# A fused retention and SiLU kernel: an early weight slice, and a two-deep pipeline for the first eight visits

## The chip, the cores and the metric

The kernel runs on one core of a Trainium2 chip. The metric is the device time of one execution in microseconds, the median of several runs. A profile of one execution gives the start and length of every instruction on the engines: TensorE (PE, with its weight loads as PEld), VectorE (DVE), ScalarE (ACT), GpSimd (POOL) and SyncE (SP), which here issues nearly all DMAs.

## The reference

Two stages follow each other. The first is a recurrent retention over 4 batches, 8 heads, 768 positions and a head dimension of 64. The second is a feed-forward layer over the resulting 3072 tokens.

```python
for t in range(S):
    state = gamma * state + k[:, :, t] (outer) v[:, :, t]
    y[:, :, t] = scale * q[:, :, t] @ state          # gamma depends on the head
x = y.transpose(0, 2, 1, 3).reshape(B * S, H * D)    # 3072 x 512
h = x @ w_in                                         # 512 x 2048
g = h * (1.0 / (1.0 + np.exp(-h)))
out = g @ w_out                                      # 2048 x 512
```

The weights arrive as 64-bit floating-point numbers, and the kernel converts them itself.

## The kernel before, in words

The recurrence is worked in chunks of 128 positions. A unit n is one chunk of one batch, in the order of chunks and within a chunk of batches, so there are 24 units, and units 0 to 3 make up chunk 0. Each unit passes through steps, and a "visit" m (the function `halves`) puts steps of several units together:

- `stage_t` (L403, L405): eight TensorE transposes of k and q, and two ScalarE copies (kt, qt) out of PSUM.
- `scale_k`: k is multiplied by its decay table gk. For units up to 5 this is one VectorE operation (L365). For units 6 to 13 it is eight ScalarE activations, one for each head (L354), since `2 * B - 3 < n < 3 * B + 2` with B = 4.
- `stage_s` (L419) and `stage_a` (L429): the state sums from scaled k and v, and the scores from kt and qt, both into the PSUM tile sc.
- `finish_a` and `scale_q`: VectorE masks the scores with the decay table (am, L437), forms mid and state (L446 or ScalarE's L444, and L450) and scales q (L370).
- `stage_y` (L462): y from the masked scores, then from the states in two halves. A small GpSimd memset stands as a fence between the halves.
- `finish_y`: ScalarE copies y out (L497) and forms the high part of x (L509). VectorE forms the two other parts (L512, L513).

In the program before, visit m holds `stage_t` and `scale_k` of unit m, the scores of unit m - 1 and y of unit m - 2: the pipeline is three deep. TensorE's order within a visit is transposes, the first part of y, sums, scores, the rest of y.

The feed-forward layer runs beside that. `product_in(c, f)` multiplies slice f of w_in (128 of its 2048 columns) with chunk c of x: twelve matmuls of 128x512 into two PSUM tiles ha and hb (L596). They use the three parts of the slice and the three parts of x, part after part. ScalarE copies ha out (L600), VectorE subtracts hb (L604), ScalarE applies Silu (L608), and g goes to DRAM.

A slice of w_in comes in three DMAs (`load_w`, L170 and L172) and is converted on its way. The 64-bit words go through ScalarE's L198 and VectorE's L200, L202, L205, L207, L209 and L215. After that come the three parts: ScalarE's L121, VectorE's L123, ScalarE's L125 and VectorE's L126. The staging tile has two buffers, so slice i + 2 can only be loaded once L209 of slice i has read its words. `take_w` converts a whole slice (slice 0 here). `begin_w` and `end_w` convert the later ones from visit 5 on, but not in visits 6 and 8. They are issued behind the newest mask:

```python
        if EARLY - 3 <= m < 3 * B + 2:
            with tc.issue_after(masked[0]):
                end_w()
                if m not in (EARLY - 2, EARLY):
                    begin_w()
```

The order of TensorE's instructions is that of the program. On the other engines a scheduler places the instructions, and each engine then works through its queue in that order. The first eight units (`EARLY = 2 * B`) are loaded at once, 24 DMAs of 256 KB each, with slices 0 and 1 between them. `make_identity`, `lag`, `decay`, `gk` and `gq` build tables on GpSimd and ScalarE at the start, some with many small memsets in `chunk_decays`.

After visit 10 has begun, the list `steps` sets the rest of the work: all further products of w_in with the remaining visits beside them, and then the products with w_out.

Of the kernel before, what the change touches and what calls it, by code (L numbers as in the profile page):

```python
# [18 lines left out]
ALU = mybir.AluOpType  # L19
# [14 lines left out]
def kernel(  # L34
# [28 lines left out]
    nc = tc.nc  # L63
    B, H, S, D = q.shape
# [65 lines left out]
    units = [(c, b) for c in range(NC) for b in range(B)]  # L130
    kqv = {"k": {}, "q": {}, "v": {}}
    EARLY = 2 * B

    FAR = 4 * B + 1
# [124 lines left out]
    for n in range(EARLY):  # L259
        for name in "kqv":  # L260
            load(name, n)
        if n in (1, 4):
            load_w(n // 4)


# [4 lines left out]
    for o in range(2):  # L270
        part = lag[ts(o, D), :D]
        nc.gpsimd.iota(part, pattern=[[1, D]], base=0, channel_multiplier=-1,
                       allow_small_or_imprecise_dtypes=True)
        nc.gpsimd.affine_select(out=part, in_=part, compare_op=ALU.is_ge, fill=1.0e6,
                                base=0, pattern=[[1, D]], channel_multiplier=-1)
    decay = const.tile([128, 2, HP, D], FP32, tag="decay", name="decay")
    for j in range(2):
        for a in range(HP):
# [24 lines left out]
    def first_chunk():  # L303
        nc.gpsimd.iota(lag, pattern=[[1, C]], base=1, channel_multiplier=0,
                       allow_small_or_imprecise_dtypes=True)
        for a in range(HP):
            nc.scalar.activation(out=gq[:, a, :], in_=lag, func=AF.Exp, scale=lgc[:, a : a + 1])

        nc.scalar.activation(out=token, in_=lgc[:1, :1], func=AF.Silu)
# [57 lines left out]
    def scale_q(n):  # L367
        c, b = units[n]
        t, g = (x if c > 0 else x[:, :, D:] for x in (qt[n], gq))
        nc.vector.tensor_tensor(out=t, in0=t, in1=g, op=ALU.mult)  # L370
# [25 lines left out]
    def stage_t(n):  # L396

        for name, to, bufs, src, tp in (
                ("kt", kt, 2, kqv["k"][n], turn(f"kp_{n}")),
                ("qt", qt, 3, kqv["q"].pop(n), banks("q", f"qp_{n}", 1)[:, 0])):  # L400
            tp = tp.rearrange("p (a t) -> p a t", a=HP)
            for a in range(HP):
                nc.tensor.transpose(tp[:, a, :], src[:, 2 * a : 2 * a + 2, :], ident)  # L403
            to[n] = one.tile([128, HP, C], FP32, tag=name, name=f"{name}_{n}", bufs=bufs)
            evac[:] = [nc.scalar.copy(out=to[n], in_=tp).ins]  # L405

    def score_tile(n):
        u = banks("s", f"sc_{n}")
        sc, sums = (u[:, :, ts(i, 4 * D)].rearrange("p o (a t) -> p o a t", a=HP)
                    for i in range(2))  # L410
        return sc, sums

    def stage_s(n, sums):

        kf, vs = kqv["k"].pop(n), kqv["v"][n]
        for a in range(HP):
            for o in range(2 if units[n][0] < NC - 1 else 1):
                for j in range(2):
                    nc.tensor.matmul(sums[ts(j, D), o, a, :], lhsT=kf[ts(o, D), 2 * a + j, :],  # L419
                                     rhs=vs[ts(o, D), 2 * a + j, :], start=True, stop=True,  # L420
                                     skip_group_check=True)

    def stage_a(n, sc):

        ktn = kt.pop(n)
        for a in range(HP):
            for o in range(2):
                for j in range(2):
                    nc.tensor.matmul(sc[ts(o, D), j, a, :], lhsT=ktn[ts(j, D), a, ts(o, D)],  # L429
                                     rhs=qt[n][ts(j, D), a, ts(o, D)], start=True, stop=True,  # L430
                                     skip_group_check=True)

    def finish_a(n, sc, sums):

        c, b = units[n]
        am[n] = one.tile([128, 2, HP, D], FP32, tag="am", name=f"am_{n}")
        mask = nc.vector.tensor_tensor(out=am[n], in0=sc, in1=decay, op=ALU.mult).ins  # L437
        masked[:] = [mask]
        mid = one.tile([128, HP, D], FP32, tag="mid", name=f"mid_{n}", bufs=2)
        steps_of[n] = state.get(b), mid  # L440

        with tc.issue_after(mask):
            if c == 0:
                nc.scalar.copy(out=mid, in_=sums[:, 0])  # L444
            else:
                nc.vector.tensor_tensor(out=mid, in0=state[b], in1=sums[:, 0], op=ALU.add)  # L446
            if c < NC - 1:
                state[b] = one.tile([128, HP, D], FP32, tag="state", name=f"state_{n}",
                                    bufs=B + 2)
                nc.vector.tensor_tensor(out=state[b], in0=mid, in1=sums[:, 1], op=ALU.add)  # L450

    def stage_y(n):

        vs, amn, qtn = kqv["v"].pop(n), am.pop(n), qt.pop(n)
        states = steps_of.pop(n)
        yp = banks("y", f"y_{n}")[:, :, : 4 * D].rearrange("p o (a t) -> p o a t", a=HP)

        started, done, new = set(), [], []

        def product(a, o, j, lhsT, rhs):  # L460
            e = j ^ (a % 2)
            i = nc.tensor.matmul(yp[ts(e, D), o, a, :], lhsT=lhsT, rhs=rhs,  # L462
                                 start=(e, o) not in started, stop=True,
                                 skip_group_check=True).ins
            started.add((e, o))
            if new:
                fence(done[-1], i)
                new.clear()
            done.append(i)

        def scores():
            for a in range(HP):
                for o in range(2):
# [12 lines left out]
        return scores, states_with, yp  # L486
# [53 lines left out]
    def visit(m):  # L540

        list(halves(m))

    def halves(m):

        first, mid, last = (0 <= m - i < len(units) for i in range(3))
        if first and m < FAR:
            stage_t(m)
        if last:
            scores, states_with, yp = stage_y(m - 2)  # L550
            scores()
            states_with(0)
        yield
        if mid:
            sc, sums = score_tile(m - 1)
            stage_s(m - 1, sums)
            stage_a(m - 1, sc)
            if 1 < m <= 3 * B + 1 and units[m - 1][1] == 0:
                next_chunk()

            with tc.issue_after(taken_out[0]) if m > 3 * B + 1 else ExitStack():
                finish_a(m - 1, sc, sums)
            scale_q(m - 1)
            if m > 3 * B + 1 and units[m - 1][1] == B - 1:

                behind_copy.append(next_chunk)
        if m == 0:
            chunk_decays()
            first_chunk()
        if first and m < FAR:  # L570
            scale_k(m)
        if last:
            states_with(1)
            finish_y(m - 2, yp)

        if FAR <= m < len(units):
            with tc.issue_after(fenced[0]):
                part_t(m)
        for name in "kqv":
            for n in (m + 1, m + 2):  # L580
                if n >= EARLY and n == (m + 1 if name == "v" or n > FAR else m + 2):
                    load(name, n)
# [28 lines left out]
    def put_g(keep):  # L611
        while len(pending) > keep:
            c, f, g = pending.pop(0)
            nc.sync.dma_start(out=g_dram[c, f], in_=g)
# [48 lines left out]
    ctx.enter_context(tc.manual_schedule(engines={mybir.EngineType.PE}))  # L663


    for m in range(EARLY + 1):
        visit(m)
        if m == 2:
            take_w()
        elif m == EARLY - 2:  # L670
            product_in(0, 0)
            load_w(3)
        elif m == EARLY:
            product_in(0, 1)
            put_g(1)
    half_visits = (x for m in range(EARLY + 1, 3 * B + 1) for x in chain(halves(m), (None,)))
    next(half_visits)
    product_in(0, 2)
    put_g(1)
    next(half_visits)  # L680
    next(half_visits)

    half = NF // 2
# [55 lines left out]
    for c in range(NC):  # L739
# [8 lines left out]
        for f in range(NF):  # L748
            n = c * NF + f
# [62 lines left out]
```

## Time and profile before

| | |
|---|---|
| time, median of 3 runs | 629.17 us (628.28 to 629.5) |
| span of the profiled execution | 625.6 us, 13502 instructions |
| ScalarE's first and VectorE's first operation with data | 2.09 us and 7.65 us |
| first product, (0,0), on TensorE | 36.24 to 39.27 us |
| second and third, (0,1) and (0,2) | 48.77 to 51.78 and 53.44 to 56.46 us |
| transposes of unit 10 | 57.71 us |

In the lines below a number of microseconds from the start of the span comes first, then the length, the engine, the line of the program, the operation and its tiles. In tables of stretches, each engine's busy time stands with its number of instructions. Where a line ends in brackets, these give how long the engine was idle before, and what it waited for last.

### The profile page before, as it was taken

To read this page: it belongs to the slowest core of one execution; us is meant where nothing else is said; L and a number is where in the kernel's file an instruction comes from. 1 tells how busy PE (TensorE), PEld (TensorE's weight loads), DVE (VectorE), ACT (ScalarE), POOL (GpSimd) and SP (SyncE) were. 2 spreads that over 40 slices of the span, in tenths; PEclk is the share of its full clock that TensorE was granted. 3 is DMA by queue.
4 is the path that set the end of the run, shared out by engine and by line. 5 is a ranking of instruction groups with operands and counts; after the bars stand their busy time and mean duration, and the time that the engine had idled before them with its cause. 6 is when DMAs were issued, how large, how long until landed. Compare 5 with 4: busy or idle time off the path is not lost.

```text
span 625.6 us, 13502 instructions
## 1 busy us (share of the span) xinstructions
PE 604.0 (97%) x5384; PEld 497.1 (79%) x5384; DVE 422.5 (68%) x729; ACT 319.5 (51%) x611; POOL 22.5 (4%) x79
## 2 busy tenths in 40 slices
PE   5888999999999999999999999999999999999997
PEld 3777787888888888888787888888788888888885
DVE  2898998698889877766698795644635453644631
ACT  6688896666665556765566871412221221313211
POOL 3000000000000211111000000000000000000000
PEclk9899999999999999999999999999999999999999
DMA  9998886446558899989566673432524432433201
GB/s 201 205 216 205 230 222 200 166 151 200 206 161 233 246 244 239 253 225 264 198 236 204 205 228 104 150 119 85 179 74 131 140 102 101 148 122 110 93 1 68
DMA packets 137999, 107.32 MB, mean 172 GB/s; under 512 B 94800, under 2 KB 103248, under 8 KB 137936
## 3 DMA queue, kind: packets, MB, share of 16 engines
q1 hardware_dynamic: 135056, 101.21, 57.4%
q10 hardware_dynamic: 2880, 5.24, 2.3%
q8 instruction: 42, 0.69, 0.5%
q14 instruction: 21, 0.17, 0.1%
HBM read 66.06 MB, written 36.70 MB: 164 GB/s over the span
## 4 chain that ended last, share of the span: by engine, by line
PE 84%; DVE 5%; SPq 5%; DMA 2%; ACT 2%; issue 1%; DVEq 0%; ACTq 0%; POOLq 0%
PE ha L596 25%; PE o L761 21%; PE oa L761 14%; PE hb L596 12%; PE ob L761 7%; SPq L150 4%; PE y L462 3%; PE sc L419 1%; PE sc L429 1%; DMA wf<-in_moe_w_out_dram 1%; DMA wf<-in_moe_w_in_dram 1%; DMA kqv<-in_k_dram 1%; DVE g L604 1%; DVE xt L512 1%; DVE cs L205 1%
## 5 line engine op out<-in xcount | busy, mean ns | idle before, releaser
L596 PE MATMUL ha<-xt,wi 128*128 128x512 f32 x768 | 193.1, 393 | 1.1 <-DVE g L604 1.0
L596 PEld LDWEIGHTS ha<-xt,wi 128*128 128x128 f32 x768 | 142.1, 188 | 32.7 <-DVE g L604 2.3
L761 PE MATMUL o<-wo,gs 128*128 128x512 f32 x576 | 146.3, 389 | 0.0
L761 PEld LDWEIGHTS o<-wo,gs 128*128 128x128 f32 x576 | 108.1, 188 | 22.4
L653 DVE TENSOR_TENSOR gs<-gr,gs 128x512 fp32r<-128x512 f32 x96 | 62.3, 686 | 85.8 <-ACT gs L651 85.8
L651 ACT ACTIVATE gs<-gr 128x512 fp32r<-128x512 f32 x96 | 53.5, 621 | 128.3 <-issue 123.6
L761 PE MATMUL oa<-wo,gs 128*128 128x512 f32 x384 | 118.4, 389 | 0.0
L596 PE MATMUL hb<-xt,wi 128*128 128x512 f32 x384 | 102.9, 390 | 0.4 <-ACT g L600 0.4
L604 DVE TENSOR_TENSOR g<-g,hb 128x512 f32<-128x512 f32 x96 | 65.7, 684 | 45.6 <-ACT g L600 29.5
L596 PEld LDWEIGHTS hb<-xt,wi 128*128 128x128 f32 x384 | 71.9, 188 | 16.0 <-ACT g L600 1.1
L761 PEld LDWEIGHTS oa<-wo,gs 128*128 128x128 f32 x384 | 72.0, 188 | 15.3 <-ACT o L769 0.3
L608 ACT ACTIVATE g<-g 128x512 f32<-128x512 f32 x96 | 60.6, 631 | 43.7 <-DVE g L604 43.3
L761 PE MATMUL ob<-wo,gs 128*128 128x512 f32 x192 | 75.3, 392 | 0.3 <-DVE o L770 0.3
L600 ACT ACTIVATE g<-ha 128x512 f32<-128x512 f32 x96 | 56.9, 592 | 29.7 <-PE ha L596 22.1
L654 DVE SCALAR_TENSOR_TENSOR gs<-gs 128x512 fp32r<-128x512 f32 x96 | 62.3, 684 | 0.1
L761 PEld LDWEIGHTS ob<-wo,gs 128*128 128x128 f32 x192 | 36.0, 188 | 9.4 <-DVE o L770 2.1
L198 ACT ACTIVATE ca<-wf 128x512 f32<-128x512 f32 x32 | 21.6, 674 | 10.4 <-DVE cs L205 5.6
L209 DVE SCALAR_TENSOR_TENSOR cp<-wf,cp 128x512 f32<-128x512 uint32 x32 | 22.8, 712 | 0.6
L769 ACT ACTIVATE o<-o 128x512 f32<-128x512 f32 x10 | 6.0, 600 | 33.4 <-PE o L761 33.0
L205 DVE SCALAR_TENSOR_TENSOR cs<-ca,cs 128x512 uint32<-128x512 uint32 x32 | 22.1, 691 | 0.8
L462 PE MATMUL y<-qt,mid 64*64 64x64 f32 x384 | 20.6, 222 | 0.0
L770 DVE TENSOR_TENSOR o<-o,o 128x512 f32<-128x512 f32 x10 | 6.8, 688 | 19.3 <-ACT o L769 19.3
(85 smaller groups left out, 568.5 us busy)
## 6 DMA issues: line engine op xcount, KB each, us to landing
gd<-g SPq DMA_DIRECT2D x96, 256.0 KB, 3.1
gr<-gd SPq DMA_DIRECT2D x96, 256.0 KB, 2.7
wf<-in_moe_w_out_dram SPq DMA_DIRECT2D x16, 512.0 KB, 4.6
out_dram<-o ACTq DMA_DIRECT2D x20, 256.0 KB, 2.1
wf<-in_moe_w_in_dram SPq DMA_DIRECT2D x16, 256.0 KB, 3.8
wf<-in_moe_w_in_dram SPq DMA_DIRECT2D x32, 128.0 KB, 3.9
kf<-in_k_dram SPq DMA_DIRECT2D x16, 256.0 KB, 5.1
qf<-in_q_dram SPq DMA_DIRECT2D x16, 256.0 KB, 3.7
```

What stands on the lines that cost most here:

```text
L150: nc.sync.dma_start(out=t, in_=src[b, :, ds(c * C, C)].rearrange("h t d -> t h d"))
L205: nc.vector.scalar_tensor_tensor(out=s, in0=a, scalar=3, in1=s, op0=ALU.logical_shift_left, op1=ALU.bitwise_or)
L209: nc.vector.scalar_tensor_tensor(out=p.bitcast(FP32), in0=lo, scalar=2.0 ** -52, in1=p.bitcast(FP32), op0=ALU.mult, op1=ALU.mult)
L462: i = nc.tensor.matmul(yp[ts(e, D), o, a, :], lhsT=lhsT, rhs=rhs, start=(e, o) not in started, stop=True, skip_group_check=True).ins
L596: nc.tensor.matmul(hb if i == 2 else ha, lhsT=w_sb[f][:, i, ts(kk, 128)], rhs=xt[c][:, i, kk, :], start=kk == 0 and i != 1, stop=kk == KIN ...
L600: copied[:] = [nc.scalar.activation(out=hs, in_=ha, func=AF.Copy, scale=ONE_E).ins]
L604: taken_out[:] = [nc.vector.tensor_tensor(out=hs, in0=hs, in1=hb, op=ALU.subtract).ins]
L608: nc.scalar.activation(out=hs, in_=hs, func=AF.Silu)
L651: nc.scalar.activation(out=t[:, 0, :], in_=g, func=AF.Copy, scale=HALF)
L653: nc.vector.tensor_tensor(out=t[:, 1, :], in0=g, in1=high, op=ALU.subtract)
L654: nc.vector.scalar_tensor_tensor(out=t[:, 2, :], in0=t[:, 1, :].bitcast(FP32), scalar=-1.0 / EPS, in1=high, op0=ALU.mult, op1=ALU.add)
L761: nc.tensor.matmul(o, lhsT=g, rhs=wo[f][:, i, :], start=first_ and i != 1, stop=last and i != 0)
```

## The change

The change reorders the start of the kernel, and the arithmetic stays as it is.

- Slice 0 of w_in is loaded behind unit 0 instead of behind unit 1, and its conversion (`take_w`) is issued after visit 0 instead of after visit 2.
- The decay tables' last input (`lagged`) is put ahead of the many memsets on GpSimd.
- For units 4 to 7 transposes and scores lie in one visit, and y comes in the visit after: two deep instead of three. A visit without a unit of its own (`at_once(None, 3, 2)`) makes the step from three to two. `soon` places `scale_k` directly behind the transposes in these visits. Visits 8 and 9 go back to three deep.
- The first products stand in visit 5 (behind the transposes, ahead of y), visit 8 (between its halves) and visit 9 (at its end). They were behind visit 6, behind visit 8 and between the halves of visit 9.

The purpose is to have x of chunk 0 ready, and the first product running, sooner. From the first half of visit 10 on, TensorE's order is the same in both programs.

```diff
-        if n in (1, 4):
+        if n in (0, 4):
             load_w(n // 4)
...
-        nc.gpsimd.affine_select(out=part, in_=part, compare_op=ALU.is_ge, fill=1.0e6,
-                                base=0, pattern=[[1, D]], channel_multiplier=-1)
+        lagged = nc.gpsimd.affine_select(out=part, in_=part, compare_op=ALU.is_ge, fill=1.0e6,
+                                         base=0, pattern=[[1, D]], channel_multiplier=-1).ins
...
+    def steps_at(m, ms=None, my=None, behind_t=None):
...
+        soon = mid and ms == m or m is None
         if first and m < FAR:
             stage_t(m)
+            if soon or m == 1:
+                scale_k(m)
+        if behind_t:
+            behind_t()
...
         if m == 0:
-            chunk_decays()
-            first_chunk()
-        if first and m < FAR:
+            with tc.issue_after(lagged):
+                chunk_decays()
+                first_chunk()
+        if first and m < FAR and not soon and m != 1:
             scale_k(m)
...
-    for m in range(EARLY + 1):
-        visit(m)
-        if m == 2:
-            take_w()
-        elif m == EARLY - 2:
-            product_in(0, 0)
-            load_w(3)
-        elif m == EARLY:
-            product_in(0, 1)
-            put_g(1)
-    half_visits = (x for m in range(EARLY + 1, 3 * B + 1) for x in chain(halves(m), (None,)))
-    next(half_visits)
+    at_once(0)
+    take_w()
+    at_once(1, 0)
+    at_once(2, 1, 0)
+    at_once(3, 2, 1)
+    at_once(None, 3, 2)
+    at_once(4, 4, 3)
+    at_once(5, 5, 4, lambda: product_in(0, 0))
+    at_once(6, 6, 5)
+    load_w(3)
+    at_once(7, 7, 6)
+    eighth = steps_at(8, None, 7)
+    next(eighth)
+    product_in(0, 1)
+    put_g(1)
+    list(eighth)
+    at_once(9, 8)
     product_in(0, 2)
     put_g(1)
-    next(half_visits)
+    half_visits = (x for m in range(EARLY + 2, 3 * B + 1) for x in chain(halves(m), (None,)))
     next(half_visits)
```

More of the change, by code (lines that the diff above doesn't have):

```diff
@@ L544, in halves @@
     def halves(m):
-        first, mid, last = (0 <= m - i < len(units) for i in range(3))
+        return steps_at(m, m - 1, m - 2)
+    def steps_at(m, ms=None, my=None, behind_t=None):
+        first, mid, last = (n is not None and 0 <= n < len(units) for n in (m, ms, my))
+        soon = mid and ms == m or m is None
         if first and m < FAR:
             stage_t(m)
+            if soon or m == 1:
+                scale_k(m)
+        if behind_t:
+            behind_t()
         if last:
-            scores, states_with, yp = stage_y(m - 2)
+            scores, states_with, yp = stage_y(my)
             scores()
@@ L554, in halves @@
         if mid:
[L555 to L558, printed above, removed]
+            sc, sums = score_tile(ms)
+            stage_s(ms, sums)
+            stage_a(ms, sc)
+            if 0 < ms <= 3 * B and units[ms][1] == 0:
                 next_chunk()
[L561 to L564, printed above, removed]
+            with tc.issue_after(taken_out[0]) if ms > 3 * B else ExitStack():
+                finish_a(ms, sc, sums)
+            scale_q(ms)
+            if ms > 3 * B and units[ms][1] == B - 1:
                 behind_copy.append(next_chunk)
         if m == 0:
-            chunk_decays()
-            first_chunk()
-        if first and m < FAR:
+            with tc.issue_after(lagged):
+                chunk_decays()
+                first_chunk()
+        if first and m < FAR and not soon and m != 1:
             scale_k(m)
@@ L573, in halves @@
             states_with(1)
-            finish_y(m - 2, yp)
+            finish_y(my, yp)
+        if m is None:
+            return
         if FAR <= m < len(units):
@@ L663, with at_once @@
     ctx.enter_context(tc.manual_schedule(engines={mybir.EngineType.PE}))
-    for m in range(EARLY + 1):
-        visit(m)
-        if m == 2:
-            take_w()
-        elif m == EARLY - 2:
-            product_in(0, 0)
-            load_w(3)
-        elif m == EARLY:
-            product_in(0, 1)
-            put_g(1)
-    half_visits = (x for m in range(EARLY + 1, 3 * B + 1) for x in chain(halves(m), (None,)))
-    next(half_visits)
+    def at_once(*of, **kw):
+        list(steps_at(*of, **kw))
+    at_once(0)
[15 more added lines that the diff above has]
+    at_once(9, 8)
     product_in(0, 2)
     put_g(1)
-    next(half_visits)
+    half_visits = (x for m in range(EARLY + 2, 3 * B + 1) for x in chain(halves(m), (None,)))
     next(half_visits)
```

## The prediction

> **What bounds the kernel now.** I read the page first, then the busy time by stretch, then the engines' timelines between 20 and 66 us. The page says what kind of kernel this is:
>
> ```profile
> PE 604.0 (97%) x5384; PEld 497.1 (79%) x5384; DVE 422.5 (68%) x729; ACT 319.5 (51%) x611; POOL 22.5 (4%) x79
> PE   5888999999999999999999999999999999999997
> DVE  2898998698889877766698795644635453644631
> ```
>
> TensorE is full from about 65 us to the end; no other engine is. So only the time at which TensorE reaches that full stretch can move the result, and whatever is won or lost before it is carried to the end. The stretches show where TensorE still has holes (columns: stretch, length, busy us and instructions of PE, weight loads, VectorE, ScalarE, GpSimd, then granted clock, DMA share, GB/s):
>
> ```profile
> 10.00:20.00 10.00, 7.71 (x193) 6.79 (x192) 5.88 (x12) 4.47 (x10) 0.09 (x1) 0.83 1.28 218
> 20.00:30.00 10.00, 7.46 (x263) 6.42 (x264) 9.48 (x19) 7.60 (x18) 0.18 (x2) 1.00 0.91 199
> 30.00:36.00 6.00, 5.00 (x227) 4.38 (x223) 5.04 (x11) 5.59 (x16) 0.35 (x2) 1.00 1.01 225
> 36.00:43.00 7.00, 7.00 (x174) 5.85 (x163) 6.93 (x14) 5.58 (x15) 0.09 (x1) 1.00 0.85 210
> 43.00:50.00 7.00, 4.06 (x136) 3.40 (x136) 6.13 (x13) 6.31 (x17) 0.09 (x1) 1.00 0.82 172
> 50.00:57.00 7.00, 7.00 (x116) 5.64 (x118) 4.79 (x10) 6.51 (x17) 0.09 (x1) 1.00 0.81 218
> 65.00:75.00 10.00, 10.00 (x185) 8.18 (x176) 9.45 (x18) 8.76 (x21) 0.09 (x1) 1.00 0.84 226
> ```
>
> The holes are before 65 us, and there VectorE (9.48 of 10, 6.93 of 7) and ScalarE (5.59 of 6, 6.31 of 7, 6.51 of 7) are nearly full. VectorE is empty mainly before 12 us. The timeline gives the marks against which I count: the scores of unit 6 masked on VectorE (mask 6 from here on) at 42.79 and those of unit 7 (mask 7) at 49.21, the third slice of w_in converted from 44.66 to 54.16, and the transposes of unit 10, the first work after which both programs issue the same instructions on TensorE, at 57.71:
>
> ```profile
> 33.85 2.03 ACT L354 ACTIVATE kqv<-kqv,gk 128x64 f32<-128x64 f32 x8
> 42.79 0.69 DVE L437 TENSOR_TENSOR am<-sc,decay 128x512 f32<-128x512 f32 x1
> 44.66 0.42 DVE L200 TENSOR_SCALAR cs<-wf 128x512 uint32<-128x512 uint32 x1
> 49.21 0.68 DVE L437 TENSOR_TENSOR am<-sc,decay 128x512 f32<-128x512 f32 x1
> 53.48 0.68 DVE L126 SCALAR_TENSOR_TENSOR wi<-wi,wil 128x512 fp32r<-128x512 f32 x1
> 56.97 0.69 DVE L604 TENSOR_TENSOR g<-g,hb 128x512 f32<-128x512 f32 x1 [2.21 <-ACT g L600]
> 57.71 0.66 PE L403 MATMUL kp<-ident,kf 128*128 128x128 f32 x4
> ```
>
> The first of these lines matters most below: the eight ScalarE scalings of k of unit 6 take 2.03 us, and today nobody waits for them, because the score product of unit 6 is a whole visit later.
>
> **What the Trainium skill says.** "Perfetto Trace Analysis", Per-engine timelines: VectorE, ScalarE and GpSimd are strict FIFO. The trace agrees: VectorE sits 2.21 us before 56.97 with other work queued behind. So an operation's place in its queue decides, and I use the instruction order of the changed program. "ScalarE: Activation LUTs", What ACT_TABLE_LOAD costs: an activation with one pointer operand costs about 280 ns + 0.833 ns an element, back-to-back ones overlapping by 93 ns; for 64 elements an estimate of 0.24 us, eight of them 1.9 us. The trace has 2.03 us, which I use. "DMA: Bandwidth & Descriptors", Why small descriptors are slow: 256-byte descriptors lose some 27%. The k, q, v rows are 256 bytes; the trace shows 199 to 225 GB/s here.
>
> **The change, part by part.** Durations are differences between consecutive starts: 0.60 us for a 128x512 VectorE operation, 0.33 for 128x256 and for the tensor-scalars; 0.47 to 0.60 for a ScalarE copy of 512; 0.95 for a unit's transposes, 0.75 and 0.38 for the two halves of y, 0.46 for the state sums, 0.42 for the scores, 2.72 for a product of 12 matmuls (2.72 us per product in the full stretch); 0.15 to 0.2 between engines.
>
> First slice and decay tables early. Removed: nothing; the bytes are the same. Slice 0 (0.5 MB, 2.3 us at 228 GB/s) passes unit 1, whose k then lands near 10.1 instead of 7.6 us. VectorE's first instruction becomes slice 0's L200, near 8.9 (today its first is unit 0's scaling at 7.65). Unit 0's scores end near 14.3 instead of 11.9 because the transposes of unit 1 stand ahead of them. Unit 2 lands at 13.2 and 14.5 as today. The tables move from 4.0 to about 2.2 on ScalarE, but the copies of unit 0 still wait for its q (6.38), so that is worth nothing. Queue order then gives mask 0 at 14.4, mask 1 at 20.4 (slice 0's L123 stands ahead of it), mask 2 at 24.4, mask 3 at 27.4, mask 4 at 31.1. Today: 12.6, 19.4, 23.6, 27.2, 31.65. So at mask 4 the change is 0.6 ahead, with unit 5 not yet transposed. The early slice pays almost nothing: VectorE idles until unit 0's scores anyway.
>
> First product at visit 5. Transposes of unit 5 at 31.0 (its q landed by 29). The product waits for x of unit 3: y3 ends 31.05, two ScalarE operations, then 33.0, VectorE's two parts ready at 33.7 and 34.9. It runs 33.0 to 35.95, against 36.24 to 39.27 today: 3.2 us earlier. But it stands ahead of y4 and of unit 5's scores, so VectorE waits for its end (34.8 to 36.1) and for the scores (36.7 to 37.95), 2.5 us that today it spends on slice 1. Mask 5 is at 37.95 (today 37.32).
>
> Visits two deep. A unit's scores now follow its transposes in the same visit, so the copy of k and q and the scaling of k lie on the path. For units up to 5 the scaling is one VectorE operation; for 6 and 7 it is ScalarE's eight. Visit 6: transposes 37.95 to 38.9; ScalarE copies until 40.3, scalings until 42.2; scores end 42.9 (visible 43.0); mask 6 stands behind slice 1's L215: 44.1 (today 42.79). Visit 7: transposes 43.2; ScalarE runs y5, a copy, x5, slice 1's L121, a copy, three scalings until 46.8, slice 1's L125 (waits for L123, 47.3) until 47.9, five scalings until 49.2; scores end 49.95; mask 7 at 50.05 (today 49.21), VectorE empty for 1.6 us before it. TensorE waits about 2.2 us for unit 6's scalings and 3.2 us for unit 7's, with no work beside them (today it loses about 2.5 us here to instruction stalls, in the trace put down to issue): y7, both products and two units' transposes are queued behind.
>
> Slice 2. Its conversion is held behind the newest mask; in visit 7 that was mask 6, now it is mask 7. L200 is at 51.95 instead of 44.66, L215 ends at 56.3. Behind it in ScalarE's queue its L121 also stands after the Silu and x7: 58.3 to 58.95, L125 to 60.5, L126 on VectorE to 60.95. Product (0,1) runs 51.85 to 54.6 (today 48.77 to 51.78); transposes and scores of unit 8 and 9 end at 56.85; product (0,2) then waits 2.1 us for slice 2 and runs 59.1 to 62.45. So unit 10's transposes come at 62.4 instead of 57.71: +4.7 us.
>
> The DMA order hides itself: slice 3 waits for slice 1's L209 (43.5 instead of 37.4), and k, q, v of units 8 to 10 queue behind it, landing by about 51 and 57.5, before their uses at 56 and 62.4. Behind unit 10 all is as before; TensorE is full, and only a few tenths of its later waits (0.3 to 0.4 at 300 to 342 us) can take any back. I take off 0.5 for these and for small errors on one side: +4.2 us, 633.4 us.
>
> **Rivals.** (a) VectorE alone decides. The work up to product (0,2)'s subtraction is the same 42.9 us of VectorE steps in both programs (three slices at 4.28, eight units at 3.06, two extra scalings 1.2, unit 8's 1.86, three subtractions 1.8, 0.7 of slice 3); today that is done at 61.4. Started at 8.9 and with only 6 us of holes it would be done at 57.8: 3.6 us faster, 625.6. For it: VectorE is the fullest engine from 20 to 45. Against: the holes I count above sum to 9 us or more. (b) ScalarE is nimbler than laid out and slice 2's wait vanishes: only visits 6 to 9 lag, +2.6 less 0.5, 631.3. For it: it is a sum of many small steps; against: the queue order is fixed. (c) The loads decide: they fill the DMA engines until 46 us in both programs (shares 0.82 to 1.28); then nothing changes, 629.2. Against: today's waits of TensorE for k and q are 4.1 us in all, most of them before 15 us.
>
> **How the numbers follow.** Main case 0.50 at 633.4; (b) 0.20 at 631.3; (c) 0.08 at 629.2; (a) 0.22 at 625.6, the other side. The main case runs to 636 if the instruction stalls of 0.5 to 1.5 us that TensorE shows today (idle put down to issue, 2.8 us on y) fall on the path too. Faster 0.22, same 0.08, slower 0.70. Range 626.0 to 636.0.
>
> **What would show it.** Right: ScalarE's scalings of units 6 and 7 end last before the state sums; mask 7 at or after 49 us, slice 2's L200 after 50 us, a TensorE wait for ScalarE's L121 before the third product, unit 10's transposes near 62 us. Wrong: mask 7 near 45 us, VectorE without holes between 30 and 50 us, unit 10's transposes before 57 us; then (a) holds.

## The result, and the profile after

| | before | after |
|---|---|---|
| time, median of 4 runs each, taken together | 628.72 us (627.94 to 629.5) | 635.07 us (634.05 to 636.01) |
| ratio after / before | | 1.011, 95% interval 1.0085 to 1.0134 |
| span of the profiled execution | 625.6 us | 634.2 us |
| first product on TensorE | 36.24 us | 34.66 us |
| mask 7 | 49.21 us | 51.84 us |
| slice 2, first VectorE step (L200) | 44.66 us | 53.71 us |
| third product on TensorE | 53.44 us | 61.60 us |
| transposes of unit 10 | 57.71 us | 65.03 us |

The change makes the kernel slower by 6.9 us by the ratio (1.1% of 628.72); the two medians lie 6.35 us apart. The purpose was met in the letter: the first product does start 1.6 us sooner. But the third starts 8.2 us later, and the end follows the third.

In the program after, the first product line of the code is L608 (L596 before), the copy and the subtraction of g are L612 and L616, and Silu is L620. The page has the same number of instructions on every engine as before:

```profile
PE 608.0 (96%) x5384; PEld 499.7 (79%) x5384; DVE 423.6 (67%) x729; ACT 319.1 (50%) x611; POOL 21.9 (3%) x79
PE   5688999999999999999999999999999999999997
DVE  2877899778979887777678797463645544554631
```

Nothing was added to any engine's work (VectorE is busy for 423.6 us against 422.5), and from the fifth slice of the span on TensorE is as full as before. So the loss lies at the start. But TensorE's busy time has grown, from 604.0 to 608.0 us: up to the transposes of unit 10 it is 47.05 of 65.03 us, against 43.33 of 57.71 us before. Of the 7.3 us between these two marks only about half is idle time. In the rest, the same instructions take longer, at a lower clock or where they follow another engine's work piece by piece (both below). The stretches say where (columns as before: stretch, length, then busy us and instructions of PE, weight loads, VectorE, ScalarE, GpSimd, then granted clock, DMA share, GB/s):

```profile
30.00:36.00 6.00, 4.13 (x110) 3.47 (x102) 5.12 (x11) 4.97 (x12) 0.09 (x1) 1.00 0.99 213
36.00:43.00 7.00, 5.73 (x190) 4.67 (x192) 4.58 (x10) 4.32 (x11) 0.09 (x1) 1.00 0.71 167
43.00:50.00 7.00, 5.02 (x162) 4.10 (x152) 6.90 (x13) 5.22 (x15) 0.18 (x2) 1.00 0.58 144
50.00:57.00 7.00, 6.99 (x133) 6.02 (x134) 5.24 (x12) 5.98 (x19) 0.09 (x1) 0.76 0.83 184
57.00:65.00 8.00, 7.00 (x106) 5.22 (x106) 5.98 (x10) 7.26 (x18) 0.00 (x0) 1.00 0.78 197
```

Between 36 and 43 us VectorE is busy for 4.58 us where it was busy for 6.93, and ScalarE for 4.32 instead of 5.58: TensorE, VectorE and ScalarE wait for each other in turn. One other thing stands in these lines: TensorE's clock is 0.76 in 50 to 57 us (it was 1.00). The timeline has the marks:

```profile
34.66 2.11 PE L608 MATMUL ha<-xt,wi 128*128 128x512 f32 x8 [0.77 <-ACT xt L509]
41.92 2.02 ACT L354 ACTIVATE kqv<-kqv,gk 128x64 f32<-128x64 f32 x8
45.91 0.68 DVE L437 TENSOR_TENSOR am<-sc,decay 128x512 f32<-128x512 f32 x1
49.63 1.29 ACT L354 ACTIVATE kqv<-kqv,gk 128x64 f32<-128x64 f32 x5
50.01 1.24 PE L419 MATMUL sc<-kqv 64*64 64x64 f32 x19 [1.15 <-ACT kqv L354]
51.84 0.69 DVE L437 TENSOR_TENSOR am<-sc,decay 128x512 f32<-128x512 f32 x1 [1.57 <-PE sc L429]
53.71 0.42 DVE L200 TENSOR_SCALAR cs<-wf 128x512 uint32<-128x512 uint32 x1
60.93 0.62 ACT L121 ACTIVATE wi<-cs 128x512 fp32r<-128x512 f32 x1
61.60 1.20 PE L608 MATMUL ha<-xt,wi 128*128 128x512 f32 x4 [0.71 <-ACT wi L121]
65.03 0.60 PE L403 MATMUL kp<-ident,kf 128*128 128x128 f32 x4
```

Read from the bottom: unit 10's transposes follow the third product, which waited for slice 2's L121 on ScalarE. That conversion began on VectorE at 53.71, behind mask 7 at 51.84. Mask 7 waited 1.57 us for the scores, these stand behind the state sums in TensorE's order, and the sums waited 1.15 us for ScalarE's scalings of k. The scalings of unit 6 take 2.02 us (2.03 before), but now the sums of the same visit need them.

A caution on single profiles, each of which is one execution. The profile after is of the slowest of its four (636.01 us). The times lie 1.8 us above the spans, so that before is of an execution of some 627.4 us, about 1 us below the median. Therefore the spans differ by 8.6 us where the medians differ by 6.35. The transposes of unit 10 also move by some 3 us with the clock that the execution was granted (experiment 1). So below the ratios decide how much, and the profiles show which wait.

The clock itself is a rival that no experiment holds fixed. The record has the mean granted clock of every execution, and one minus this clock, times the span, is an estimate of the most that half clock can have cost (where TensorE waits anyway, it costs nothing). Averaged over the executions of each program it comes to about 2 us before, 2.2 to 2.9 us in the experiments that are three deep throughout (1, 9 and 11), 5.2 us in the change, and 3.3 to 6.9 us in the others. So up to some 3 us of the loss may be the lower clock that comes after waits, and not the waits themselves.

### The profile page after: what moved, and what is told of

It is laid out like the page before. It is cut to its first block, busy times and chain, and to the rows that moved or that the text cites. A ratio compares the mean times of both kernels' runs of the same rounds, so it can differ in the third digit from the quotient of the medians.

```text
span 634.2 us, 13499 instructions
## 1 busy us (share of the span) xinstructions
PE 608.0 (96%) x5384; PEld 499.7 (79%) x5384; DVE 423.6 (67%) x729; ACT 319.1 (50%) x611; POOL 21.9 (3%) x79
## 4 chain that ended last, share of the span: by engine, by line
PE 80%; DVE 7%; DMA 5%; ACT 5%; issue 2%; SPq 0%; DVEq 0%; ACTq 0%; POOLq 0%
PE ha L608 22%; PE o L781 20%; PE oa L781 14%; PE hb L608 11%; PE ob L781 7%; PE y L462 3%; PE sc L429 1%; DMA qw<-qp 1%; PE sc L419 1%; DVE g L616 1%; DMA gd<-g 1%; DMA wf<-in_moe_w_out_dram 1%; PE qp L403 1%; DVE cp L209 1%; PE kp L403 1%
## 5 line engine op out<-in xcount | busy, mean ns | idle before, releaser
L608 PE MATMUL ha<-xt,wi 128*128 128x512 f32 x768 | 193.4, 394 | 3.2 <-DVE g L616 1.0
L608 PEld LDWEIGHTS ha<-xt,wi 128*128 128x128 f32 x768 | 142.1, 188 | 35.5 <-DVE g L616 2.4
L608 PE MATMUL hb<-xt,wi 128*128 128x512 f32 x384 | 103.3, 391 | 0.4 <-ACT g L612 0.2
L616 DVE TENSOR_TENSOR g<-g,hb 128x512 f32<-128x512 f32 x96 | 65.6, 684 | 48.7 <-ACT g L612 35.9
L608 PEld LDWEIGHTS hb<-xt,wi 128*128 128x128 f32 x384 | 71.7, 188 | 16.8 <-ACT g L612 1.8
L620 ACT ACTIVATE g<-g 128x512 f32<-128x512 f32 x96 | 60.5, 630 | 44.6 <-DVE g L616 44.4
L612 ACT ACTIVATE g<-ha 128x512 f32<-128x512 f32 x96 | 56.7, 590 | 33.5 <-PE ha L608 19.8
L437 DVE TENSOR_TENSOR am<-sc,decay 128x512 f32<-128x512 f32 x24 | 16.5, 686 | 9.6 <-PE sc L429 9.6
```

What stands on the lines that cost most here:

```text
L608: nc.tensor.matmul(hb if i == 2 else ha, lhsT=w_sb[f][:, i, ts(kk, 128)], rhs=xt[c][:, i, kk, :], start=kk == 0 and i != 1, stop=kk == KIN ...
L612: copied[:] = [nc.scalar.activation(out=hs, in_=ha, func=AF.Copy, scale=ONE_E).ins]
L616: taken_out[:] = [nc.vector.tensor_tensor(out=hs, in0=hs, in1=hb, op=ALU.subtract).ins]
L620: nc.scalar.activation(out=hs, in_=hs, func=AF.Silu)
```

## The experiments

Each ratio is to the program before on the same chip. The change itself stands at 1.0110 (1.0085 to 1.0134), that is +6.9 us. From these intervals, a difference between the change and an experiment is uncertain by nearly 2 us.

**1. The early slice alone.** The program before with slice 0 behind unit 0, its conversion after visit 0, and the tables ahead of the memsets. The pipeline is three deep everywhere.

```diff
-        if n in (1, 4):
+        if n in (0, 4):
...
-        if m == 2:
+        if m == 0:
             take_w()
```

> The visits, products and their order of the kernel before, three deep, with only the early slice 0 (load behind unit 0, conversion after visit 0) and the decay tables put ahead. Theory (the early slice pays almost nothing, since VectorE is empty until unit 0's scores anyway): within 1 us of the kernel before, 628 to 630 us, unit 10's transposes within 1 us of 57.7. Rival (VectorE's early start is worth what it frees later): 3 us faster, unit 10's transposes at 55 us or sooner.

Measured: 628.73 us against 628.32, ratio 1.0005 (0.9994 to 1.0016). The early slice and the early tables cost 1.0 us at most and bring 0.4 us at most. The mark was a miss: unit 10 is transposed at 61.07 us, 3.4 later than in the profile of the program before. The profiled execution took 630.03 us, 1.3 above the median of this run. TensorE's clock in it is 0.50 from 47 to 53 us, where the profile before has 1.00; with the edges it is 6.8 us at half, which is 3.4 us of work lost. In the waits of its TensorE from 20 to 66 us (engine, line, what it waited for: total us, times, longest) little but instruction stalls and the wait for ys is left, beside two waits of 0.3 and 0.2 us:

```profile
PE y L462 <- issue: 4.6, 4, 1.5
PE y L462 <- ACT ys L497: 2.3, 1, 2.3
PE qp L403 <- issue: 1.8, 1, 1.8
```

The 2.3 us for ys are at the place where slice 0's L121 and L125 now stand ahead in ScalarE's queue. The wait is real, and the ratio says that the end does not feel it here.

**2. The scalings of k of units 6 and 7 on VectorE.** One operation in place of eight activations.

```diff
-            if 2 * B - 3 < n < 3 * B + 2:
+            if 2 * B - 1 < n < 3 * B + 2:
```

> The changed kernel, with k of units 6 and 7 scaled by one VectorE operation each instead of eight ScalarE activations. Theory (the ScalarE scalings stand on the path of the two-deep visits): TensorE no longer waits for L354 before the state sums of unit 7, which end near 49 instead of 51.3 us; unit 10's transposes near 63 instead of 65.0; about 2 us faster than the changed kernel, near 633. Rival (the order of the loads or the place of the first product is the cause): no gain, and 1.2 us more of VectorE work to pay, 635 to 636.

Measured: 633.16 us against 628.32, ratio 1.0075 (1.0055 to 1.0094). The time is as expected, but the interval overlaps that of the change. TensorE still waits for the scalings, on the other engine:

```profile
PE sc L419 <- DVE kqv L365: 2.3, 2, 1.8
```

VectorE's queue was not empty in front of the scaling either, so the wait was moved, and only part of it removed.

**3. Slice 2 begun a visit sooner.** It is begun behind mask 6 again, and slice 3's load is issued ahead of it.

```diff
-                if m not in (EARLY - 2, EARLY):
+                if m not in (EARLY - 1, EARLY):
...
-    at_once(6, 6, 5)
     load_w(3)
+    at_once(6, 6, 5)
```

> The changed kernel, with the conversion of slice 2 begun in visit 6, behind mask 6, instead of in visit 7, behind mask 7. Theory (slice 2 comes late for the third product): L200 of slice 2 near 50 instead of 53.7 us, TensorE's waits for L121 and L125 before the third product (1.0 us together) gone, 1 to 1.5 us faster than the changed kernel, near 634. Rival: the time lies in the visits alone, no gain, 635.

Measured: 632.29 us against 628.32, ratio 1.0068 (1.0048 to 1.0088), whose upper end just meets the interval of the change. The gain is more than was expected. Slice 2's L200 is at 50.26 us, unit 10 at 63.83, and the third product no longer waits for the slice at all. The wait for slice 2 was part of the loss; experiment 6 shows it apart from the change.

**4. Both of these.** The edits of 2 and 3 together.

> Both edits together: k of units 6 and 7 scaled on VectorE and slice 2 begun in visit 6. Theory: the gains add, 3 to 4 us faster than the changed kernel, 631 to 632, unit 10's transposes near 61. Rival (VectorE is the bound once the waits are gone): no more than the better one of the two alone, 633.

Measured: 634.47 us against 628.32, ratio 1.0097 (1.0079 to 1.0114). This is a miss: it is no better than either edit alone. VectorE's timeline shows a cause (L123 and L126 belong to slice 1, L200 to slice 2, L365 is the scaling of unit 7):

```profile
49.54 0.68 DVE L123 SCALAR_TENSOR_TENSOR wil<-cs,wi 128x512 f32<-128x512 f32 x1
50.15 0.68 DVE L513 SCALAR_TENSOR_TENSOR xt<-xt 128x512 fp32r<-128x512 f32 x1
50.75 0.68 DVE L126 SCALAR_TENSOR_TENSOR wi<-wi,wil 128x512 fp32r<-128x512 f32 x1
51.35 0.42 DVE L200 TENSOR_SCALAR cs<-wf 128x512 uint32<-128x512 uint32 x1
51.69 0.68 DVE L365 TENSOR_TENSOR kqv<-kqv,gk 128x512 f32<-128x512 f32 x1
...
54.80 0.68 DVE L437 TENSOR_TENSOR am<-sc,decay 128x512 f32<-128x512 f32 x1
```

With slice 2 begun a visit sooner, VectorE's queue holds conversion steps of both slices ahead of unit 7's scaling. The scaling waits behind work for products of the next visits, and TensorE behind the scaling: in the waits of this run it is 4.1 us for L365, where experiment 2 had 2.3. Mask 7 comes at 54.80 us, later than in the change itself. A second cause is not excluded: in this profile TensorE is at half clock for some 10 us between 43 and 58 us, while in experiment 2's the clock stays at 1.00 from 30 to 65 us. Over all executions the estimate from the mean clock is 6.9 us here, against 4.6 and 4.8 us in experiments 2 and 3.

**5. The scalings on GpSimd.** The rival was that VectorE's queue, with slice 2 behind mask 7, is the only cause, and that the scalings don't matter. If they do, and it is queues that hold them up, an engine with an empty queue must do better.

```diff
-            if 2 * B - 3 < n < 3 * B + 2:
+            if 2 * B - 1 < n < 3 * B + 2:
...
-            nc.vector.tensor_tensor(out=t, in0=t, in1=g, op=ALU.mult)
+            on = nc.gpsimd if 2 * B - 3 < n < 2 * B else nc.vector
+            on.tensor_tensor(out=t, in0=t, in1=g, op=ALU.mult)
```

> The changed kernel, with k of units 6 and 7 scaled by one GpSimd operation each, whose queue holds nothing but the fences there. Theory (the wait for the scalings is one of two causes): no TensorE wait for L354 before the sums of unit 7 and, unlike on VectorE, no queue ahead of it; if the operation takes less than 1.5 us, 2 to 3 us faster than the changed kernel, 632 to 633. Rival (the queue of VectorE, with slice 2 behind mask 7, is the only cause): no gain, 634 to 635.

Measured: 631.63 us against 627.92, ratio 1.0061 (1.0045 to 1.0077), apart from that of the change. GpSimd's timeline (L366 is L365 in the program after):

```profile
40.73 1.04 POOL L366 TENSOR_TENSOR kqv<-kqv,gk 128x512 f32<-128x512 f32 x1 [1.60 <-PE kp L404]
45.78 1.44 POOL L366 TENSOR_TENSOR kqv<-kqv,gk 128x512 f32<-128x512 f32 x1 [1.59 <-PE kp L404]
```

It starts as soon as the transposes are done and is slow (1.04 and 1.44 us, against 0.68 on VectorE), but nothing stands ahead of it. No wait for kqv stands among TensorE's waits in this profile. So the scalings cost some 3 us of the 6.9 (1.0110 less 1.0061, times 628; with both intervals, 1.2 to 4.9). It is also better than experiment 2, but their intervals overlap.

**6. Both slices a visit sooner.** Experiment 3, and slice 1 too.

```diff
-        if EARLY - 3 <= m < 3 * B + 2:
+        if EARLY - 4 <= m < 3 * B + 2:
...
-                if m not in (EARLY - 2, EARLY):
+                if m not in (EARLY - 3, EARLY - 1, EARLY):
```

> The changed kernel, with slices 1 and 2 both begun a visit sooner (slice 1 in visit 4 behind mask 4, slice 2 in visit 6 behind mask 6), which is behind the same masks as in the kernel before. Theory (the two-deep order holds each slice back by one mask, which is the larger part of the loss): slice 1's L200 near 34 instead of 41.5 us, VectorE's idle 2.4 us around the first product filled, slice 2's near 47 instead of 53.7, unit 10's transposes 61 to 62; 630.5 to 631.5 us, 1 to 2 us better than with slice 2 alone. Rival (what is left after slice 2 is the waits for the ScalarE scalings alone): no better than with slice 2 alone, 632 to 633.

Measured: 631.82 us against 627.92, ratio 1.0059 (1.0045 to 1.0072), apart from the change. Slice 1's L200 moves from 41.52 to 35.31 us, slice 2's to 48.27. Unit 10 is at 63.44 us, which misses the 61 to 62 expected and is hardly sooner than in experiment 3 (63.83). Against experiment 3 no gain can be measured, as the rival had it. Slice 2's place costs some 3 us, and slice 1's shows no cost of its own.

**7. Slices sooner and scalings on GpSimd** (5 and 6 together).

> Both of the last two edits: the slices behind the masks of the kernel before, and k of units 6 and 7 scaled on GpSimd. Theory (these two are all of the loss): 628 to 630 us, the same as the kernel before or slightly faster, unit 10's transposes at 57 to 59. Rival (something in the two-deep order itself remains, such as the visit without a unit, or the TensorE clock that falls where it idles): 631 or more.

Measured: 629.93 us against 627.92, ratio 1.0029 (1.0016 to 1.0041). Now the gains nearly add: 0.0049 and 0.0051 alone, 0.0081 together. Three quarters of the loss is undone with the pipeline two deep and the first product at visit 5. The mark expected for unit 10 was missed (62.43 us). In this profile the second product's first part takes 3.64 us for eight matmuls, where the first product's eight took 2.11 in the program after. The stretches around it:

```profile
48.00:50.00 2.00, 0.94 (x8) 0.63 (x6) 1.93 (x5) 1.55 (x3) 0.00 (x0) 1.00 0.94 200
50.00:52.00 2.00, 0.75 (x33) 0.59 (x32) 2.00 (x4) 0.78 (x2) 0.00 (x0) 1.00 0.34 99
52.00:54.00 2.00, 1.83 (x19) 1.48 (x20) 2.00 (x5) 1.84 (x7) 0.09 (x1) 0.62 0.84 262
54.00:56.00 2.00, 2.00 (x6) 1.60 (x5) 0.85 (x2) 0.55 (x2) 0.00 (x0) 0.52 0.79 197
```

TensorE is busy for less than half of 48 to 52 us, and then granted about half its clock for 4 us. What remains of the loss, 1.8 us, would fit that, but it was not tried apart and stays open.

**8. The pipeline two deep only for units 4 and 5**, or **only for 6 and 7.** In the first the visit without a unit stays where it was, and from visit 6 on the scores are again a visit later. In the second the first product stands behind visit 6.

```diff
-    at_once(6, 6, 5)
+    at_once(6, None, 5)
     load_w(3)
-    at_once(7, 7, 6)
-    eighth = steps_at(8, None, 7)
-    next(eighth)
+    at_once(7, 6)
+    at_once(8, 7, 6)
...
```

> The changed kernel up to visit 5, with its early slice and its first product there; from visit 6 on three deep again, second and third product where the kernel before has them. Theory (the loss lies in visits 6 and 7, where the ScalarE scalings stand on the path, and in slice 2 held behind mask 7): most of the loss returns, 629 to 630 us, no TensorE wait for L354 before the sums of unit 7, slice 2's L200 before 48 us, unit 10's transposes at 57 to 60. Rival (the two-deep visits 3 to 5 or the early first product cost as much): 632 or more.

```diff
-    at_once(None, 3, 2)
-    at_once(4, 4, 3)
-    at_once(5, 5, 4, lambda: product_in(0, 0))
+    at_once(4, 3, 2)
+    at_once(5, 4, 3)
+    at_once(None, 5, 4)
     at_once(6, 6, 5)
+    product_in(0, 0)
```

> Three deep to visit 5, then an extra visit, and units 6 and 7 two deep as in the change; first product behind visit 6. Theory: the loss of the change is here alone, 633 to 636 us, with the TensorE wait for L354 before the sums of unit 7 and slice 2's L200 after 50 us. Rival (the loss needs visits 3 to 5 two deep): 630 or less.

Measured: 630.65 us against 627.42, ratio 1.0053 (1.0039 to 1.0067), for units 4 and 5; 632.42 against 627.42, ratio 1.0068 (1.0043 to 1.0093), for units 6 and 7. The first lies between what theory and rival expected, and missed both its marks (slice 2's L200 at 49.22 us, where before 48 was expected, and unit 10 at 61.00 us, where 57 to 60 was). The second is just under its range. Each half costs by itself, 3.3 and 4.3 us. That of units 6 and 7 has the causes above (slice 2's L200 is at 53.38 us, and its L121 is waited for 1.1 us). In units 4 and 5 no ScalarE scaling is involved, and something else must cost. TensorE's waits in the first of the two:

```profile
PE y L462 <- ACT ys L497: 3.0, 2, 2.3
PE y L462 <- DVE am L437: 2.0, 1, 2.0
PE y L462 <- ACT qt L405: 1.4, 1, 1.4
```

The longest is that for ys, but the same wait of 2.3 us stands in experiments 1 and 9, whose ratios are 1.0005 and 1.0014. The waits for a mask and for the copy of q stand in neither of these two, so they are the likelier cause. Which of them reaches the end was not taken apart.

**9. Three deep all along, with the early slice and the early product.** Product (0,0) stands in visit 6, between the transposes and y.

```diff
-    at_once(None, 3, 2)
-    at_once(4, 4, 3)
-    at_once(5, 5, 4, lambda: product_in(0, 0))
-    at_once(6, 6, 5)
+    at_once(4, 3, 2)
+    at_once(5, 4, 3)
+    at_once(6, 5, 4, lambda: product_in(0, 0))
     load_w(3)
-    at_once(7, 7, 6)
+    at_once(7, 6, 5)
+    at_once(8, 7, 6)
...
```

> Three deep all along, with the early slice and tables, and the first product placed in visit 6 between the transposes and y of unit 4, which is the place in the visit that the change gave it. Theory (the place of the first product is a small matter): within 1.5 us of the kernel before, 628 to 630. Rival (the product ahead of y holds VectorE up): 2 us or more slower, 630.5 or more.

Measured: 629.24 us against 627.42, ratio 1.0014 (0.9998 to 1.0029). The product runs at 34.2 us, as early as in the change, and the cost is at most 1.8 us. So the early product and the early slice don't make the bulk of the loss, and the depth does.

**10. The first product behind visit 5** instead of ahead of y.

```diff
-    at_once(5, 5, 4, lambda: product_in(0, 0))
+    at_once(5, 5, 4)
+    product_in(0, 0)
```

> The changed kernel, with the first product moved from the middle of visit 5 to behind it. Theory: VectorE's two waits there (1.4 us for the product's end, 1.1 us for unit 5's scores) shrink and mask 5 comes near 37 instead of 39.7 us, but visits 6 and 7 still wait for ScalarE, so 1 to 2 us faster than the changed kernel, 633 to 634. Rival (the first product's place is the main cause): 4 us faster or more, 631 or less.

Measured: 633.41 us against 627.42, ratio 1.0087 (1.0064 to 1.0109). Mask 5 comes at 36.73 us instead of 39.66. The time is as expected, but its interval overlaps that of the change, so the product's place within the visit is not shown to matter.

**11. The program before with k of units 6 to 8 scaled on GpSimd.**

```diff
-            if 2 * B - 3 < n < 3 * B + 2:
+            if 2 * B < n < 3 * B + 2:
...
-            nc.vector.tensor_tensor(out=t, in0=t, in1=g, op=ALU.mult)
+            on = nc.gpsimd if 2 * B - 3 < n < 3 * B + 2 else nc.vector
+            on.tensor_tensor(out=t, in0=t, in1=g, op=ALU.mult)
```

> The kernel before, three deep, with k of units 6, 7 and 8 scaled by one GpSimd operation each (1.0 to 1.4 us in the run with GpSimd) instead of eight ScalarE activations. Theory (three deep, nobody waits for the scalings, and ScalarE's queue is not the end of the chain): within 1.5 us of the kernel before, 626.5 to 629. Rival (ScalarE, full to nine tenths from 43 to 57 us, is what the start waits for): 2 to 3 us faster, 625 to 626, a version that beats both.

Measured: 628.28 us against 627.66, ratio 1.0005 (0.9992 to 1.0018). With three deep nobody waits for the scalings, and freeing ScalarE of them brings nothing. It is the counterpart of experiment 5: nearly the same edit is worth 3 us or nothing, depending on whether the sums come in the same visit. No version was found that beats the program before.

## Why the prediction was right, and where its sum was off

**Direction and cause: right.** The forecast was +4.2 us. Measured are +6.9 by the ratio and +6.35 between the medians, inside the range. The signs it named are all there: the scalings of unit 7 end last before its state sums, mask 7 is after 49 us, slice 2's L200 after 50, the third product waits for L121, unit 10 is transposed after 62. Rival (a), VectorE alone decides, falls: VectorE had the holes that were counted (1.57 us before mask 7, 1.6 predicted). Rival (c), the loads decide, falls with the time itself. Rival (b), slice 2's wait vanishes, falls as well, since TensorE waited 0.71 us for L121 and 0.28 for L125.

**Units 4 and 5: not foreseen.** The prediction put mask 4 at 0.6 us ahead of the program before and mask 5 at 0.6 behind, and put nearly all of the loss into visits 6 and 7 and slice 2. Its 4.2 us are close to the 4.3 that units 6 and 7 cost alone in experiment 8. The 3.3 us of units 4 and 5 are missing from its sum. That the total is inside the range all the same is partly luck, since the upper end had been set for instruction stalls.

| mark, us | predicted | after | off by |
|---|---|---|---|
| mask 2 | 24.4 | 24.57 | +0.2 |
| mask 3 | 27.4 | 28.47 | +1.1 |
| mask 4 | 31.1 | 32.77 | +1.7 |
| mask 5 | 37.95 | 39.66 | +1.7 |
| mask 6 | 44.1 | 45.91 | +1.8 |
| mask 7 | 50.05 | 51.84 | +1.8 |
| slice 2, L200 | 51.95 | 53.71 | +1.8 |
| product (0,1) | 51.85 | 55.33 | +3.5 |
| slice 2, L126 ends | 60.95 | 63.56 | +2.6 |
| product (0,2) | 59.1 | 61.60 | +2.5 |
| transposes of unit 10 | 62.4 | 65.03 | +2.6 |

**The early slice "pays almost nothing".** Shown by experiment 1 (1.0005).

**Mask 3 and 4: the term that was too small.** The step "queue order then gives mask 3 at 27.4, mask 4 at 31.1" is 1.7 us early. From there to mask 7 every distance was right to about 0.1 us, so this is one error carried on. Where it arises, TensorE's timeline shows:

```profile
21.25 1.13 PE L462 MATMUL y<-am,kqv 64*64 64x64 f32 x32 [2.30 <-ACT ys L497]
26.89 0.34 PE L462 MATMUL y<-am,kqv 64*64 64x64 f32 x6 [0.78 <-issue]
31.32 0.33 PE L462 MATMUL y<-qt,mid 64*64 64x64 f32 x4 [1.10 <-ACT qt L405]
```

The longest of these waits, 2.30 us for the copy of y behind slice 0's L121 and L125 on ScalarE, is not to blame: mask 2 comes after it, and was only 0.2 us late. From mask 2 to mask 3 the program took 0.9 us more than predicted, and there TensorE stands for 0.78 us in an instruction stall. In the first program of experiment 8, whose order is the same up to here, there is no stall at this place, and the distance is 3.0 us, as predicted. From mask 3 to mask 4 it took 0.6 us more, and there TensorE waits 1.10 us for ScalarE's copy of q, which stands behind the copies of y, k and mid and behind x in that queue. The prediction named such stalls as what could carry its main case to 636 us, but put none into the sum. That these two make up the 1.7 us is argued from the marks, and how much of it reaches the end is not shown.

**The first product.** It came at 34.66 instead of 33.0, by the same 1.7 us. Whether its place ahead of y costs anything, experiment 10 could not show.

**The scalings of k on the path.** Right, and shown: experiment 5 takes them away for 3 us, and experiment 11 shows that they are free three deep. The sum wrote 2.2 and 3.2 us of TensorE's waits to them. In the profile only 1.15 us, at unit 7, are put down to L354. At unit 6 TensorE stood for 1.27 us in an instruction stall while the scalings ran, and its sums then followed them head by head. The skill's statement that the prediction leaned on, strict FIFO on VectorE, ScalarE and GpSimd ("Perfetto Trace Analysis", Per-engine timelines), is what experiments 2, 4 and 5 come down to. The traces agree: in experiment 4 unit 7's scaling starts at 51.69 us, behind the operations queued before it, though the transposes of k had ended at 47.74.

**Slice 2.** Right, and shown: moving it gives back some 3 us (experiment 6). Its L200 came 1.8 us late, as everything did, and its end 2.6 us late. L121 stood in ScalarE's queue until 60.93 us behind Silu and x7, as foreseen. These came late because product (0,1) and the second half of y7 did. The third product's wait for it, predicted as 2.1 us, shrank to about 1 us, since TensorE was late as well.

**TensorE's clock: not in the sum.** Product (0,1) is 1.7 us later than the 1.8 carried on explain, and the stretches of the program after show why:

```profile
48.00:50.00 2.00, 0.84 (x14) 0.58 (x10) 2.00 (x4) 1.40 (x6) 0.09 (x1) 1.00 0.93 212
52.00:54.00 2.00, 2.00 (x14) 1.67 (x16) 2.00 (x5) 1.49 (x3) 0.00 (x0) 0.50 0.54 157
54.00:56.00 2.00, 2.00 (x51) 1.78 (x52) 1.89 (x5) 2.00 (x8) 0.09 (x1) 0.67 1.17 256
```

After a stretch with TensorE busy for 0.84 of 2 us, its clock is 0.50, and unit 8's transposes take 1.12 us for four instead of 0.66. The prediction knew that TensorE would wait there, and priced the waits but not the clock that follows. At unit 10 about half of this is hidden: it is 2.6 us late, 0.8 more than the 1.8 carried on. TensorE would have waited for slice 2 anyway, but slice 2's L121 is later too, since it stands behind the Silu of product (0,1).

**What comes back later.** The prediction let later waits take back 0.5 us. The profile shows none of it: from the sixth product to the 48th the subtractions of g come 7.5 to 8.1 us later than before, where unit 10 was 7.3 late. But these are two single executions whose spans lie 2 us further apart than the medians, so whether the usual execution takes anything back stays open. One further loss of this profile, 2.59 us of ScalarE's wait for a DMA of g, was not foreseen:

```profile
75.65 0.60 ACT L612 ACTIVATE g<-ha 128x512 f32<-128x512 f32 x1 [2.59 <-DMA gd<-g]
```

In experiment 3's profile it is missing, so it hangs on timing. A step of about 1.5 us more near 211 to 221 us stands in this one profile and in none of the other programs at this place (experiment 5's has one of 1.8 us near 245 us). What it is stays open.

**What stays open:** the 3.3 us of units 4 and 5 two deep (experiment 8), the last 1.8 us after the repairs (experiment 7), and how much of the loss is the clock.

## What to carry to other kernels

A shallower pipeline puts on the path what the deeper one hid: not only the operations themselves but the queues of the helper engines that they pass through, so walk every in-order queue between a transpose and its use before taking a stage out. Work hung on "behind the newest mask" moves with the depth of the pipeline, and has to be placed again when the depth changes. Before an operation is moved to another in-order engine, look at what stands in that queue: with slice 2 begun sooner, the ratio was 1.0097 with the scalings on VectorE (experiment 4), and 1.0029 with them on GpSimd, the slower engine (experiment 7, with slice 1 sooner too).

## What the runs showed of the hardware

- Half the clock was granted after waits that are far from complete idleness. In the program after TensorE was busy for 0.84 of 2 us (48 to 50 us), and for 2.27 of the last 3.42 us ahead of the drop. Its clock in single microseconds from 51 to 56 us was then 0.96, 0.50, 0.50, 0.50 and 0.84, which makes 3.4 us at half. In experiment 7 (0.94 and 0.75 of 2 us in turn) it was 3.4 us as well, and in experiment 1 6.8 us. The Trainium skill ("TensorE: Matmul & The Clock Gate", What's actually happening) has the clock gate with two states, full and half, decided over windows of about 3.4 us that run freely. The traces agree in the 0.50 and in the length. The values between, such as 0.62 and 0.67 over 2 us, are stretches that hold both states. The same section puts half clock after an idle window; here TensorE was busy for two thirds of one. At which busy share the clock falls stays open.
- It does not come each time: in experiment 5's profile TensorE was busy for only 0.91 of 2 us (46 to 48 us), and the clock stayed at 1.00 from 43 to 65 us. In experiments 2 and 4 TensorE had nearly the same two waits between 41 and 45 us (0.99 and 1.78, 1.02 and 1.75 us); the clock stayed at 1.00 in the first and fell to 0.50 in the second.
- A multiply of 128x512 in fp32 on GpSimd took 1.04 to 1.53 us (experiments 5, 7 and 11). The Trainium skill ("GPSIMD Engine Reference", 3.1 Elementwise — side-by-side cycle accounting) has 4.50 us for an add of 2048 elements. A quarter of that, an estimate of 1.12 us, is near the shortest. VectorE was busy throughout beside both multiplies of experiment 5 (1.04 and 1.44 us), so that alone doesn't explain the difference. VectorE was held up too: its scaling of q (L371), otherwise 0.68 us, took 1.49, 0.85 and 1.43 us where a GpSimd multiply ran beside it. The cause was not tried.
- TensorE's stalls that are put down to issue vary widely between profiles and say little of the time: from 20 to 66 us they are 6.4 us in experiment 1 (628.73 us) and 0.6 us in the first of experiment 8 (630.65 us).
